# Attention with mixed heads and a gated feed-forward: Keys loaded three places further ahead, and two of four score evictions on VectorE

## The chip, the cores and the metric

The kernel runs on one core of one Trainium2 chip. The metric is the device time in microseconds (us) of one execution, and the time before is the median of 3 runs: 1879.54 us (1875.44 to 1880.68).

## What is computed

Eight batches of 448 tokens with 12 heads of 64. Scores are mixed over the heads before the softmax, and its result is mixed over the heads again before it meets the Values. The attention's output, 3584 rows of 768, goes through a feed-forward layer with a gate.

```python
scores = scale * np.matmul(q, k.transpose(0, 1, 3, 2))
scores = np.einsum('bhij,hg->bgij', scores, w_pre)
scores = scores - np.max(scores, axis=-1, keepdims=True)
attn = np.exp(scores)
attn = attn / (np.sum(attn, axis=-1, keepdims=True) + 1e-09)
attn = np.einsum('bhij,hg->bgij', attn, w_post)
out = np.matmul(attn, v)
x = out.transpose(0, 2, 1, 3).reshape(B * S, H * D)
h = x @ w_in
g = h - np.tanh(h)
return g @ w_out
```

## The kernel before

The kernel has two stages. In the attention stage each batch's 448 queries are four blocks (120, 120, 120 and 88 rows), and each block is cut into groups of ten queries. A group has 120 rows, one for each of its queries and each head, so that both mixes over heads are matmuls with a block-diagonal matrix of 120 x 120. Two groups at a time make a *place*: the stage is a loop of some 180 places (`for p in range(NPL + 3)`), each of which does this:

- **gather**: SyncE issues two DMAs (line 496) that collect the scores of two groups from the tile `s` into tiles `t`, for two places later. `t` has three buffers for even groups and two for odd ones.
- **issue** (line 370): behind the gathers SyncE issues up to six DMAs that wait in a list: loads of Queries, Keys and Values, stores of finished x, and, last, chunks of the weights that are being converted. A load that is put on the list in one place is issued in the next one. SyncE issues in order and waits in order.
- **premix** (lines 512 to 517): TensorE mixes two groups into two banks `ps_p`, the second one from a high part `th` and a low part `tl` of `t`.
- **norm** (541 to 545): VectorE takes the reciprocals of the last place's sums, ScalarE scales the mix matrix by them (`wr`).
- **split** (504, 505): VectorE casts the next place's odd group to `th`, GpSimd makes `tl`.
- **expo** (527, 529): VectorE's maxima, behind the cast in its order, and ScalarE's exponentials `e`. They release `ps_p` for the next premix.
- **jobs of this place**, from the table `todo`: transposes of Keys (`prep_k`, line 415) or Queries (`prep_q`, 441) on TensorE, values (line 598), or the scores of two pairs of heads (line 475). All of them share four banks `ps_m`. Their evictions are put behind the exponentials: line 481 for scores, 426 and 427 for Keys, 454 and 456 for Queries.
- **mix** (557) of the last place; ScalarE evicts it into `at` (566) at the start of the next place.
- a step or two of the **conversion** of the weights (lines 80 to 104) on VectorE, ScalarE and GpSimd.

A fixed order is recorded for each engine; nothing is reordered at run time. Scores of one pair of heads fill two banks; `scores` is called for an even pair `hp` and then for the odd one, so that a score place fills four banks and has four evictions. Before, an even pair's go to ScalarE and VectorE, and an odd pair's both to ScalarE. The first 16 evictions name their engines themselves and are not touched.

The table `todo` is filled by a planner ahead of the loop. For each batch but the first it chooses three places `p` for the loads of Keys (four heads each, 448 KB, pieces of 256 bytes; two buffers `kr`) and for each a place `o` for its transposes: at least two places after `p`, never in a place with scores or transposed Queries, and for the second and third load not before the score places that free a buffer of the transposed Keys. The third load waits for the first one's transposes, whose buffer it takes. Loads and transposes come out of it as follows (place of load, place of transposes; the load is issued one place after its own), from place 0 on:

| batch | first | second | third |
|---|---|---|---|
| 1 | 5, 7 | 6, 11 | 8, 13 |
| 2 | 27, 30 | 28, 34 | 31, 36 |
| 3 | 50, 52 | 51, 56 | 53, 58 |
| 4 | 72, 75 | 73, 79 | 76, 81 |
| 5 | 95, 97 | 96, 101 | 98, 103 |
| 6 | 117, 120 | 118, 124 | 121, 126 |
| 7 | 140, 142 | 141, 146 | 143, 148 |

The Values of the next batch are loaded at the places around these (in batch 2 at 26, 27 and 28), as are a Query block and the store of x.

The second stage is the feed-forward layer (lines 249 to 321), which the change does not touch.

Of the kernel before, what the change touches and what calls it, by code (L numbers as in the profile page):

```python
# [148 lines left out]
def kernel_body(  # L149
# [11 lines left out]
    nc = tc.nc  # L161
# [121 lines left out]
    def parts_gate(r):  # L283
        z = r.shape[1]
        gh = ff.gp.tile([P, TB], F32R, name="gh", tag="gh")
        gl = ff.gp.tile([P, TB], F32R, name="gl", tag="gl")
        nc.scalar.copy(gh[:, :z], r)  # L287
        nc.vector.tensor_sub(gl[:, :z], r, raw(gh[:, :z]))  # L288
        return gh, gl
# [47 lines left out]
    with ExitStack() as st:  # L337
# [16 lines left out]
        blocks = [(b, m) for b in range(B) for m in range(NM)]  # L354
# [110 lines left out]
        def scores(i, hp, engines=None):  # L465

            b, m = blocks[i]
            n = sizes[m]
            if hp == 0:
                sts[i] = sp.tile([MT, H, S], F32, name="s", tag="s")  # L470
            (qh, ql), (kh, kl) = qbs[i], kks[b, hp // 2]
            pss = [ps_m.tile([P, 512], F32, name="ps_q", tag="ps_m") for _ in halves]
            for x, (qx, kx) in enumerate(((qh, kh), (qh, kl), (ql, kh))):
                for a, ps in zip(halves, pss):
                    nc.tensor.matmul(ps[:n, :S], qx[a, hp, :], kx[a, hp % 2], start=(x == 0), stop=(x == 2))  # L475

            def rest():

                two = engines or (nc.scalar.copy, nc.scalar.copy if hp % 2 else nc.vector.tensor_copy)
                for j, (eng, ps) in enumerate(zip(two, pss)):  # L480
                    eng(sts[i][:n, 2 * hp + j, :], ps[:n, :S])

            sooner.append(rest)
# [252 lines left out]
        first = [t for t, (i, g) in enumerate(groups) if g == 0] + [NG, NG, NG]  # L736
        todo = {p: [] for p in range(NPL + 8)}

        def at_place(p, *job):
            todo[p].append(job)  # L740
# [13 lines left out]
        at_s, p, kind = {}, 0, None  # L754
# [18 lines left out]
        for i, (b, m) in enumerate(blocks):  # L773
            p0 = first[i] // 2
            if i + 2 < len(blocks):
                p = at_s[i + 2, 0] - 1
# [5 lines left out]
                for hq in range(NP // 2):  # L782
                    at_place(p0 + 4 + hq, load_v, b, hq)
        for b in range(1, B):
            p, o, done = first[blocks.index((b - 1, 1))] // 2 - 1, 0, []
            for hq in range(3):
                if hq == 2:

                    p = max(p, done[0] + 1)
                at_place(p, load_k, b, hq)  # L790
                o = max(p + 2, o + 1)
                p += 1
                if hq > KB - 4:

                    o = max(o, at_s[blocks.index((b - 1, 3)), hq - 1 - (KB - 4)] + 1)
                for r in range(2):
                    while any(f is scores or f is prep_q for f, *a in todo[o]):
                        o += 1
                    at_place(o, prep_k, b, 2 * hq + r)
                done.append(o)  # L800
                assert o < at_s[blocks.index((b, 0)), hq], (b, hq)
# [69 lines left out]
    for n in range(N):  # L871
        b, f = n // NF, n % NF
# [13 lines left out]
        if n + 3 == N:  # L886
            done = {n + 1: [parts_gate(gates.pop(n + 1))]}
# [48 lines left out]
```

## Time and profile before

| | |
|---|---|
| median of 3 runs | 1879.54 us (1875.44 to 1880.68) |
| the profiled execution, its own time | 1880.95 us |
| its span, first to last instruction | 1879.2 us |
| mean granted TensorE clock | 0.998 of full speed |
| attention stage, first premix to the last mix | 24 to 936 us |
| feed-forward stage | 936 to 1879 us |

The profile is of one execution. Busy time is given by engine: PE is TensorE's matmuls, PEld its loads of weights, DVE VectorE, ACT ScalarE, POOL GpSimd, SP SyncE; SPq are the DMAs that SyncE issues. An arrow names what an engine waited for by engine, tile and line; a wait for several things is put down to the one that came last by the profile, and where the engine named had long been done, it was another, often a DMA. Matmuls are pipelined, and their ends are modelled. Rows of a timeline begin with start and length in us; rows of stretches have the window, its length, the busy times of PE, PEld, DVE, ACT and POOL with their instructions, the granted clock, the DMA engines' share and GB/s.

### The profile page before, as it was taken

The numbers are of one execution on the slowest core, as the hardware profiler recorded it, in microseconds if no ns is written. First come the engines' busy times: TensorE is split into PE (matmuls) and PEld (weight loads), VectorE is DVE, ScalarE is ACT, GpSimd is POOL, SyncE is SP. The second block draws the span as 40 slices with busy tenths as digits, with TensorE's granted clock in tenths as the row PEclk, the third lists the DMA queues.
The fourth block names the chain that finished last, engine by engine and source line by source line (L and its number), as shares of the span: only waits on it lengthen the run. The fifth ranks groups of instructions, "written<-read, shape, count | busy, mean of one in ns | idle before, by whom it ended". The sixth has DMA issues, their size and how long they took to land.

```text
span 1879.2 us, 35344 instructions
## 1 busy us (share of the span) xinstructions
PE 1851.1 (99%) x13150; PEld 1525.9 (81%) x13150; DVE 1184.7 (63%) x2457; ACT 1133.8 (60%) x2503; POOL 451.9 (24%) x401
## 2 busy tenths in 40 slices
PE   8999999999999999999999999999999999999998
PEld 6777887787878777877788888888888888888887
DVE  5676766767776676766456556556566566565555
ACT  5787887878888788788634443434434434433433
POOL 2344444444444345444201000000000000000000
PEclk9999999999999999999999999999999999999999
DMA  6667658676675757656565565665655655655651
GB/s 162 183 183 201 189 166 221 182 208 190 177 216 171 209 177 205 195 164 189 212 255 193 206 246 192 223 218 196 235 213 196 235 205 196 237 209 191 233 193 42
DMA packets 232795, 371.92 MB, mean 198 GB/s; under 512 B 98992, under 2 KB 207536, under 8 KB 218288
## 3 DMA queue, kind: packets, MB, share of 16 engines
q1 hardware_dynamic: 231740, 368.45, 60.5%
q8 instruction: 104, 1.70, 0.4%
q10 hardware_dynamic: 884, 1.22, 0.2%
q14 instruction: 67, 0.55, 0.1%
HBM read 245.37 MB, written 47.19 MB: 156 GB/s over the span
## 4 chain that ended last, share of the span: by engine, by line
PE 86%; DMA 6%; ACT 3%; DVE 2%; issue 2%; POOL 1%; SPq 0%; ACTq 0%; POOLq 0%; DVEq 0%
PE ps_o L557 13%; PE ps_h L256 8%; PE ps_h L260 8%; PE ps_h L255 8%; PE ps_m L598 7%; PE ps_p L512 6%; PE ps_q L475 6%; PE ya L303 5%; PE ya L300 5%; PE ya L301 5%; DMA t<-s 4%; PE yb L303 3%; PE yb L301 3%; PE yb L300 3%; PE ps_p L517 2%
## 5 line engine op out<-in xcount | busy, mean ns | idle before, releaser
L557 PEld LDWEIGHTS ps_o<-wr,e 120*112 120x112 f32 (+1 forms) x2880 | 307.2, 177 | 49.8 <-issue 30.1
L557 PE MATMUL ps_o<-wr,e 120*112 120x120 f32 (+1 forms) x2880 | 340.5, 271 | 4.1 <-ACT wr L545 4.1
L527 DVE TENSOR_REDUCE mx<-ps_p 120x1 f32<-120x448 f32 x360 | 218.6, 622 | 136.9 <-PE ps_p L512 136.7
L505 POOL TENSOR_TENSOR tl<-t,th 120x448 fp32r<-120x448 f32 x179 | 204.4, 1142 | 391.8 <-DVE th L504 221.5
L287 ACT CAST gh<-r 128x512 fp32r<-128x512 f32 x112 | 69.6, 621 | 373.3 <-DVE r L280 373.3
L256 PE MATMUL ps_h<-xl,w 128*128 128x512 f32 x672 | 263.2, 392 | 0.5 <-POOL pad L222 0.5
L255 PE MATMUL ps_h<-xh,w 128*128 128x512 f32 x672 | 262.8, 391 | 0.0
L529 ACT ACTIVATE e<-ps_p,mx 120x448 f32<-120x448 f32 x360 | 225.8, 636 | 36.7 <-DVE mx L527 36.1
L245 POOL TENSOR_TENSOR xl<-rx,xh 128x512 fp32r<-128x512 f32 x38 | 53.7, 1415 | 741.3 <-ACT xh L244 741.3
L566 ACT COPY at<-ps_o 112x960 f32<-112x960 f32 x156 | 154.5, 990 | 113.4 <-PE ps_o L557 112.5
L303 PE MATMUL ya<-w,gl 128*128 128x512 f32 x448 | 177.1, 395 | 0.7 <-DVE gl L288 0.7
L276 DVE SCALAR_TENSOR_TENSOR r<-qa,ps_h 128x512 f32<-128x512 f32 x112 | 77.0, 687 | 158.7 <-ACT t L273 158.7
L300 PE MATMUL ya<-w,gh 128*128 128x512 f32 x448 | 175.0, 391 | 1.3 <-ACT gh L287 1.3
L301 PE MATMUL ya<-w,gh 128*128 128x512 f32 x448 | 174.9, 390 | 0.0
L260 PE MATMUL ps_h<-xh,w 128*128 128x512 f32 x672 | 170.5, 389 | 0.0
L512 PE MATMUL ps_p<-t,wpre 120*120 120x448 f32 x360 | 165.7, 542 | 4.3 <-ACT e L529 3.5
L598 PE MATMUL ps_m<-at,vr 112*64 112x120 f32 (+1 forms) x3072 | 163.3, 263 | 1.9 <-ACT at L566 1.5
L598 PEld LDWEIGHTS ps_m<-at,vr 112*64 112x64 f32 x3072 | 149.7, 138 | 14.7 <-ACT at L566 3.7
L270 ACT ACTIVATE u<-ps_h 128x512 f32<-128x512 f32 x112 | 66.9, 597 | 149.2 <-PE ps_h L260 149.2
L260 PEld LDWEIGHTS ps_h<-xh,w 128*128 128x128 f32 x672 | 126.1, 188 | 26.2
L256 PEld LDWEIGHTS ps_h<-xl,w 128*128 128x128 f32 x672 | 126.6, 188 | 24.6 <-POOL pad L222 0.9
L255 PEld LDWEIGHTS ps_h<-xh,w 128*128 128x128 f32 x672 | 126.6, 188 | 22.9
(102 smaller groups left out, 3622.0 us busy)
## 6 DMA issues: line engine op xcount, KB each, us to landing
w<-ws SPq DMA_DIRECT2D x112, 1536.0 KB
t<-s SPq DMA_DIRECT2D x342, 210.0 KB
cr<-in_moe_w_in_dram SPq DMA_DIRECT2D x24, 512.0 KB
cr<-in_moe_w_out_dram SPq DMA_DIRECT2D x32, 384.0 KB
vr<-in_v_dram SPq DMA_DIRECT2D x24, 448.0 KB
kr<-in_k_dram SPq DMA_DIRECT2D x23, 448.0 KB
out_dram<-ob SPq DMA_DIRECT2D x24, 384.0 KB
qr<-in_q_dram SPq DMA_DIRECT2D x23, 360.0 KB
```

Source lines behind the costliest of these rows:

```text
L255: nc.tensor.matmul(ph, wh[:, fs], xh, start=(c == 0), stop=False)
L256: nc.tensor.matmul(ph, wh[:, fs], xl, start=False, stop=False)
L260: nc.tensor.matmul(ph, wl[:, fs], xh, start=False, stop=(c == NK - 1))
L300: nc.tensor.matmul(y, gh[:, tok], wh[:, es], start=first, stop=False)
L301: nc.tensor.matmul(y, gh[:, tok], wl[:, es], start=False, stop=False)
L303: nc.tensor.matmul(y, gl[:, tok], wh[:, es], start=False, stop=last)
L505: eng.tensor_sub(tl[:n, :], x[:n, :], raw(th[:n, :]))
L512: nc.tensor.matmul(pa[:n, :], wpre[:n, :n], tg.pop(2 * p)[:n, :], start=True, stop=True)
L527: nc.vector.tensor_reduce(out=mx[:n, :], in_=ps[:n, :], axis=AX.X, op=ALU.max, negate=True)
L529: nc.scalar.activation(e[:n, :], ps[:n, :], AF.Exp, bias=mx[:n, :], scale=1.0, accum_out=zs[:n, 0, j : j + 1])
L557: nc.tensor.matmul(ps[:CP, j, c * GP : (c + 1) * GP], e[:n, c * CP : (c + 1) * CP], wr[:n, j, :], start=True, stop=True,)
L598: nc.tensor.matmul(pv[j * D : (j + 1) * D, r, :n], vt[:, j, c, :], ats[i][:, c, 2 * hp + j, :n], start=(c == 0), stop=(c == NC - 1),)
```

## The change

The loads of Keys are planned from three places earlier, transposes come at least four places after their load, and an odd pair's second score eviction goes to VectorE.

```diff
             def rest():
-
-                two = engines or (nc.scalar.copy, nc.scalar.copy if hp % 2 else nc.vector.tensor_copy)
+                two = engines or (nc.scalar.copy, nc.vector.tensor_copy)
                 for j, (eng, ps) in enumerate(zip(two, pss)):
                     eng(sts[i][:n, 2 * hp + j, :], ps[:n, :S])
...
         for b in range(1, B):
-            p, o, done = first[blocks.index((b - 1, 1))] // 2 - 1, 0, []
+            p, o, done = first[blocks.index((b - 1, 1))] // 2 - 4, 0, []
             for hq in range(3):
                 if hq == 2:
                     p = max(p, done[0] + 1)
                 at_place(p, load_k, b, hq)
-                o = max(p + 2, o + 1)
+                o = max(p + 4, o + 1)
                 p += 1
```

The table becomes:

| batch | first | second | third |
|---|---|---|---|
| 1 | 2, 7 | 3, 11 | 8, 13 |
| 2 | 24, 28 | 25, 34 | 29, 36 |
| 3 | 47, 52 | 48, 56 | 53, 58 |
| 4 | 69, 73 | 70, 79 | 74, 81 |
| 5 | 92, 97 | 93, 101 | 98, 103 |
| 6 | 114, 118 | 115, 124 | 119, 126 |
| 7 | 137, 142 | 138, 146 | 143, 148 |

Of the transposes only the first ones of batches 2, 4 and 6 move. Lines from 479 on have one number less after the change (a blank line went).

SyncE near the start of the attention stage, before: `t` are gathers, `kr` Keys, `qr` a Query block, `cr` chunks of weights.

```order
L496 DMA t<-s 120x1x448 x14
L367 DMA qr<-in_q_dram 88x12x64
L367 DMA cr<-in_moe_w_in_dram 128x1024 x3
L496 DMA t<-s 120x1x448 x2
L367 DMA kr<-in_k_dram 112x16x64
L496 DMA t<-s 120x1x448 x2
L367 DMA kr<-in_k_dram 112x16x64
L496 DMA t<-s 120x1x448 x4
L367 DMA kr<-in_k_dram 112x16x64
```

The same stretch after:

```order
L495 DMA t<-s 120x1x448 x10
L367 DMA kr<-in_k_dram 112x16x64
L495 DMA t<-s 120x1x448 x2
L367 DMA kr<-in_k_dram 112x16x64
L495 DMA t<-s 120x1x448 x2
L367 DMA qr<-in_q_dram 88x12x64
L367 DMA cr<-in_moe_w_in_dram 128x1024 x3
L495 DMA t<-s 120x1x448 x8
L367 DMA kr<-in_k_dram 112x16x64
```

The first two Keys' loads of batch 1 now stand ahead of the Query block and the weights, and of two more pairs of gathers each; the third stands where it stood.

TensorE at place 28, before: premix (`ps_p`), mix (`ps_o`) and the next premix.

```order
L512 MATMUL ps_p<-t,wpre 120x448
L515 MATMUL ps_p<-th,wph 120x448
L516 MATMUL ps_p<-th,wpl 120x448
L517 MATMUL ps_p<-tl,wph 120x448
L557 MATMUL ps_o<-wr,e 112x120 x8
```

And after:

```order
L511 MATMUL ps_p<-t,wpre 120x448
L514 MATMUL ps_p<-th,wph 120x448
L515 MATMUL ps_p<-th,wpl 120x448
L516 MATMUL ps_p<-tl,wph 120x448
L415 MATMUL ps_m<-ident,kr 128x112 x8
L556 MATMUL ps_o<-wr,e 112x120 x8
```

The transposes of the first Keys of batch 2 came from place 30, where they stood ahead of that place's values.

VectorE in a score place, before: the maxima (`mx`), one eviction (`s`), two kinds of conversion steps, and the next place's normalisation (`zs`).

```order
L527 TENSOR_REDUCE mx<-ps_p 120x1 x2
L481 COPY s<-ps_q 120x448
L80 TENSOR_SCALAR cm<-cr 128x512 x2
L83 TENSOR_SCALAR cr<-cr 128x512 x2
L541 TENSOR_SCALAR zs<-zs 120x1 x2
```

And after:

```order
L526 TENSOR_REDUCE mx<-ps_p 120x1 x2
L480 COPY s<-ps_q 120x448 x2
L80 TENSOR_SCALAR cm<-cr 128x512 x2
L83 TENSOR_SCALAR cr<-cr 128x512 x2
L540 TENSOR_SCALAR zs<-zs 120x1 x2
```

A second eviction stands between the maxima and the conversion; on ScalarE two stand where three did.

## The prediction

> **What bounds the kernel now.** I read the page first. TensorE is busy for nearly the whole span, so what can be won is its idle time and any time at a lower clock.
>
> ```profile
> PE 1851.1 (99%) x13150; PEld 1525.9 (81%) x13150; DVE 1184.7 (63%) x2457; ACT 1133.8 (60%) x2503; POOL 451.9 (24%) x401
> ```
>
> Of 1879.2 us, 28.1 are idle. The waits of TensorE's matmuls, longest in total first, say for what:
>
> ```profile
> PE ps_o L557 <- ACT wr L545: 4.1, 7, 1.3
> PE ps_m L415 <- DMA kr<-in_k_dram: 3.9, 3, 1.4
> PE ps_p L512 <- ACT e L529: 3.5, 5, 0.9
> PE ps_m L415 <- ACT e L529: 3.3, 1, 3.3
> PE ps_m L598 <- ACT at L566: 1.5, 2, 1.3
> ```
>
> Columns: us in total, times, longest. L415 is the transposes of Keys; four of their waits, 7.2 us together, are the two rows with L415. The row of 3.3 names an exponential of ScalarE, which the transposes do not need: they need banks that earlier evictions have emptied, and Keys in SBUF. A wait for several things is put down to the one seen last, so I take it for the load as well. TensorE's timeline around it (start, us, then the idle time in brackets):
>
> ```profile
> 52.74 0.92 PE L512 MATMUL ps_p<-t,wpre 120*120 120x448 f32 x2
> ...
> 57.53 1.73 PE L415 MATMUL ps_m<-ident,kr 112*128 112x112 f32 x8 [3.26 <-ACT e L529]
> 59.18 4.84 PE L598 MATMUL ps_m<-at,vr 112*64 112x120 f32 x48
> ...
> 65.68 0.92 PE L512 MATMUL ps_p<-t,wpre 120*120 120x448 f32 x2
> ```
>
> Four batches later the same work of one place (premix, transposes, values, mix) met its Keys in time:
>
> ```profile
> 516.41 0.92 PE L512 MATMUL ps_p<-t,wpre 120*120 120x448 f32 x2
> ...
> 518.64 2.68 PE L598 MATMUL ps_m<-at,vr 112*64 112x120 f32 x48
> ...
> 522.98 0.92 PE L512 MATMUL ps_p<-t,wpre 120*120 120x448 f32 x2
> ```
>
> From premix to premix that is 65.68 - 52.74 = 12.94 us against 522.98 - 516.41 = 6.57: the late Keys cost 6.37, of which 3.26 is the gap. The rest is the clock, as the stretches show (after POOL's busy time come the granted clock, the DMA share and GB/s):
>
> ```profile
> 57.00:64.00 7.00, 6.47 (x57) 6.07 (x57) 2.26 (x5) 3.28 (x8) 0.39 (x1) 0.53 0.70 170
> 64.00:70.00 6.00, 6.00 (x49) 4.87 (x48) 4.44 (x11) 4.10 (x10) 1.13 (x1) 1.00 0.21 70
> 280.00:290.00 10.00, 8.58 (x65) 6.62 (x62) 6.96 (x20) 7.57 (x20) 3.71 (x3) 1.00 1.08 267
> 740.00:750.00 10.00, 8.93 (x82) 6.93 (x77) 6.45 (x19) 8.93 (x22) 5.09 (x5) 1.00 1.00 259
> ```
>
> After the gap of 3.26 us the clock was 0.53 for 7 us; at the shorter gaps (up to 1.4 us, at 289 and 749 us) it stayed 1.00. The Trainium skill, "TensorE: Matmul & The Clock Gate", Part 1, says that the clock halves after an idle window of about 3.4 us that runs freely, so that a gap of this size may or may not trip it. The trace agrees that it can; in a run where it does not, the time before would be about 3 us shorter, and the time after the same.
>
> **Part 1, the loads.** Before, SyncE issued the second batch's first Keys behind a Query block and three chunks of weights:
>
> ```profile
> 43.83 0.62 SPq L367 DMA_DIRECT2D qr<-in_q_dram  x1
> 44.50 1.65 SPq L367 DMA_DIRECT2D cr<-in_moe_w_in_dram  x3
> ...
> 48.00 0.65 SPq L367 DMA_DIRECT2D kr<-in_k_dram  x1
> ```
>
> They were awaited at 57.53, 9.5 us later. In the new order two Keys' loads stand ahead of that Query block, and there are four places to the transposes, some 18 us at the 4.59 us of a score place (below); some places are shorter. For the later batches the load leaves the crowded stretch (with Values, Query, and the write of x) for one three places earlier:
>
> ```profile
> 170.00:180.00 10.00, 10.00 (x101) 8.11 (x100) 5.75 (x16) 8.25 (x22) 4.51 (x5) 1.00 1.09 237
> 150.00:160.00 10.00, 10.00 (x106) 8.24 (x108) 6.76 (x19) 7.81 (x21) 4.29 (x4) 1.00 0.49 147
> ...
> 380.00:390.00 10.00, 10.00 (x108) 8.11 (x106) 5.93 (x19) 8.37 (x21) 4.28 (x4) 1.00 0.38 133
> ```
>
> There the DMA engines are at 0.38 to 0.49 instead of 1.00 to 1.09. In the even batches the first transposes also move two places up, so their distance grows by one place only; three places after its issue are some 14 us, and 9.5 was enough in the crowded stretch. So all four waits go: 3.26 + 3.9 = 7.2 us, and 12.94 - 6.57 - 3.26 = 3.1 us of halved clock. Sum 10.3.
>
> Is something else late next at 54 us? Its neighbours:
>
> ```profile
> 55.73 0.39 DVE L504 CAST th<-t 120x448 fp32r<-120x448 f32 x1 [2.90 <-DMA t<-s]
> 56.26 1.13 POOL L505 TENSOR_TENSOR tl<-t,th 120x448 fp32r<-120x448 f32 x1 [6.38 <-DVE th L504]
> 57.38 0.62 ACT L529 ACTIVATE e<-ps_p,mx 120x448 f32<-120x448 f32 x1
> ```
>
> The gather was late as well, but the next premix, at 52.74 + 6.57 = 59.31, finds its operand (56.26 + 1.13 = 57.39) and its bank (57.38 + 0.62 = 58.00) ready. Nothing takes the place of the wait.
>
> What the moved loads cost where they now stand: each is ahead of the next two gathers in SyncE's order, and a late gather holds VectorE at L504:
>
> ```profile
> DVE th L504 <- DMA t<-s: 50.2, 25, 5.6
> ```
>
> That is 2.0 us a time. TensorE's non-Keys waits are 4.1 + 3.5 + 1.5 = 9.1 us, so at most 18% of those 50.2 us can have reached it. 17 loads move (two a batch in seven batches, and the third of the three even ones by two places). From below: nothing, as with third Keys' loads, of which five already stand by themselves and left TensorE busy through the 14 us behind each; one of these, and one of the two that did not:
>
> ```profile
> 189.11:203.11 14.00, 14.00 (x127) 11.27 (x125) 11.49 (x30) 13.18 (x34) 5.57 (x6) 1.00 0.86 239
> 299.49:313.49 14.00, 12.85 (x122) 10.32 (x120) 9.39 (x23) 9.79 (x24) 7.71 (x7) 1.00 0.83 214
> ```
>
> From above: 17 x 2.0 x 0.18 = 6.1 us at the trace's own share, 34 if all of it passed. I take 0, since the other loads that made 299 us hard are no neighbours any more; the old places lose the same number of loads.
>
> The transposes that move (batches 2, 4, 6) come into a place without values, where ScalarE's two casts have less room. Seven such places (the second Keys of a batch) exist already; two had a wait behind them:
>
> ```profile
> 313.47 0.36 PE L557 MATMUL ps_o<-wr,e 120*112 120x120 f32 x1 [1.15 <-ACT wr L545]
> 542.87 0.64 PE L512 MATMUL ps_p<-t,wpre 120*120 120x448 f32 x1 [0.40 <-ACT e L529]
> ```
>
> So 3 x (1.15 + 0.40) / 7 = 0.7 us, between 0 and 3 x 1.15 = 3.5. I take 0.7.
>
> **Part 2, the evictions.** Eight score places use a pair of engines of their own; 92 others now send the second odd eviction to VectorE.
>
> ```profile
> L481 ACT COPY s<-ps_q 120x448 f32<-120x448 f32 (+1 forms) x284 | 132.3, 544 | 6.5 <-PE ps_q L475 6.2
> L481 DVE COPY s<-ps_q 120x448 f32<-120x448 f32 (+1 forms) x100 | 62.0, 621 | 16.8 <-PE ps_q L475 16.3 <-DMA ws<-cs 0.4
> ```
>
> ScalarE loses 132.3 / 284 = 0.47 us of busy time a score place, VectorE gains 0.62 (92 x 0.62 = 57 us). The Trainium skill, "VectorE: DVE Perf Modes", Specifications, puts ScalarE closer to PSUM and VectorE closer to SBUF, which speaks against this half; the rows agree, 544 ns against 621. Who has room is read from two score places, premix to premix:
>
> ```profile
> 112.91:117.50 4.59, 4.59 (x34) 3.47 (x33) 2.97 (x8) 4.59 (x13) 4.13 (x4) 1.00 0.96 234
> 342.89:347.48 4.59, 4.59 (x34) 3.47 (x33) 2.97 (x9) 4.59 (x12) 1.77 (x3) 1.00 1.00 223
> ```
>
> ScalarE has none (4.59 of 4.59), VectorE is at 2.97 and goes to 3.6. The cost of 57 us is thus covered by VectorE's idle time there. Behind both places TensorE waited for ScalarE:
>
> ```profile
> 118.56 0.36 PE L557 MATMUL ps_o<-wr,e 120*112 120x120 f32 x1 [0.48 <-ACT wr L545]
> 348.43 0.36 PE L557 MATMUL ps_o<-wr,e 120*112 120x120 f32 x1 [0.38 <-ACT wr L545]
> ```
>
> 0.47 us less on ScalarE ends such waits: 0.48 + 0.38 = 0.9. Two more waits stood where Keys and Values were loaded together:
>
> ```profile
> 186.36 0.64 PE L512 MATMUL ps_p<-t,wpre 120*120 120x448 f32 x1 [0.65 <-ACT e L529]
> 647.18 0.64 PE L512 MATMUL ps_p<-t,wpre 120*120 120x448 f32 x1 [0.95 <-ACT e L529]
> ```
>
> With the Keys gone from there I count these 1.6 as won, too. So 2.5 us of the 9.1; the bounds are 0 and 9.1.
>
> **Sum.** The profiled execution took 1880.95 us (span 1879.2, and 1.75 around it), 1.4 above the median of 1879.54. 1880.95 - 10.3 - 2.5 + 0.7 = 1868.85, so 1868.9 us. I leave the 1.4 out: what differs between the runs (1875.44 to 1880.68) is of the size of the clock's 3.1 us, which the change ends.
>
> **Rivals.** (a) *The loads only move the collision.* The Keys land in time, but the gathers behind the 17 of them come late, VectorE stands at L504, its maxima and ScalarE's exponentials slip, and premix waits. For it: score places and places with values of 4.6 to 5.8 us now follow the loads, no longer ones. Against it: the row at 189.11. At 18% it gives 1880.95 - 10.3 + 6.1 = 1876.8. If all 34 us passed it would be 1880.95 - 10.3 + 34 = 1904.7, slower. It ends the gain from 10.3 / 34 = 30% on, and is slower by 0.3% from (10.3 + 5.6) / 34 = 47% on. Chance 15%; 4 of these slower.
> (b) *VectorE becomes the bound in score places.* Its order is in sequence: two evictions stand ahead of the next normalisation, cast and maximum. For it: 3.6 of 4.59 us is a mean of engines that wait for each other. If a third of the 0.62 us came through at 92 places it would be 92 x 0.2 = 18 us: 1880.95 - 10.3 + 18 = 1888.7. Against it: ScalarE at 4.59 of 4.59 lost under 0.5 us a time. Chance 4%.
> (c) *The loads are not early enough in the even batches.* Then the gap of 1.44 us at 636 stays: 1870.3. Chance 4%; inside the range.
>
> **Numbers.** A difference of 0.3%, 5.6 us, is about what a measurement of this kernel can tell: faster is under 1873.9, slower over 1885.1. Forecast with (c): 81%, a few of these above 1873.9. Range: the low end if all 9.1 us of other waits go, 1880.95 - 10.3 - 9.1 = 1861.6; the high end is rival (a) at its 18% with the 0.7 of the transposes, 1877.5. So 1862 to 1877.5. Faster 0.77, same 0.16, slower 0.07.
>
> **What would show it.** Right: no wait of L415 for kr, the place at 53 us 6.6 us long, clock 1.00 from 50 to 70 us, L481 at 192 copies each on ScalarE and VectorE, the matmuls' waits for wr shorter. Wrong: L504 waiting for t well over 50.2 us and L512 waiting for e over 5 us (a), or score places longer than 4.6 us with VectorE at their length (b).

## The result, and the profile after

The changed kernel took 1861.18 us, the median of 4 runs (1859.88 to 1861.98), against 1877.49 (1875.19 to 1880.68) for the kernel before: a ratio of 0.9911, 95% interval 0.9892 to 0.993. That is faster, as forecast, and 0.8 us under the low end of the range (1862.0). The forecast was a gain of 12.1 us on the profiled execution. By the medians the gain is 16.3 us. Between the two profiled executions it is 21.0 (spans of 1879.2 and 1858.2 us), but that sets an execution of before that is slower than its median beside the fastest of the changed kernel.

The page's engine row of the profile after (the one of before stands in the prediction):

```profile
PE 1844.0 (99%) x13150; PEld 1523.0 (82%) x13150; DVE 1230.1 (66%) x2549; ACT 1099.2 (59%) x2411; POOL 455.4 (25%) x401
```

TensorE's idle time fell from 28.1 to 1858.2 - 1844.0 = 14.2 us. Its busy time fell as well, by 7.1 us, though it issued the same 13150 matmuls: 3.1 us of it by the prediction's reading is time at half the clock. The other 4.0 I take for waits that the view of busy time does not show as idle.

The matmuls' waits after (lines from 479 on have one number less):

```profile
PE ya L300 <- ACT gh L287: 1.9, 2, 1.0
PE ps_o L556 <- ACT wr L544: 1.6, 2, 1.3
PE ps_b L658 <- POOL ident masks.py:199: 1.5, 1, 1.5
PE ps_p L511 <- ACT e L528: 0.9, 1, 0.9
```

No transposes (L415) wait for Keys any more. Of the 9.1 us of other waits in the attention stage (for `wr`, `e` and `at`) 2.5 are left: the two rows with `ps_o` and `ps_p`. All but 0.3 of that are two waits, of 0.9 us at the stage's second place and 1.3 at its end, that stood there before as well.

TensorE's timeline at the place that took 12.94 us before:

```profile
53.06 0.92 PE L511 MATMUL ps_p<-t,wpre 120*120 120x448 f32 x2
...
54.43 0.93 PE L415 MATMUL ps_m<-ident,kr 112*128 112x112 f32 x8
55.29 2.68 PE L597 MATMUL ps_m<-at,vr 112*64 112x120 f32 x48
...
59.63 0.92 PE L511 MATMUL ps_p<-t,wpre 120*120 120x448 f32 x2
```

59.63 - 53.06 = 6.57 us, and no idle time in front of the transposes. (The first two Keys' loads passed three pairs of gathers each, not the two that the description of the change gives.) The clock over the same stretches as before:

```profile
57.00:64.00 7.00, 7.00 (x67) 5.72 (x64) 6.42 (x16) 6.50 (x17) 2.22 (x2) 1.00 0.18 71
64.00:70.00 6.00, 6.00 (x75) 5.24 (x74) 5.21 (x17) 3.99 (x11) 3.94 (x4) 1.00 0.69 187
```

It is 1.00 where it was 0.53. VectorE's wait for the gathers, and the score evictions by engine:

```profile
DVE th L503 <- DMA t<-s: 28.1, 19, 3.4
```

```profile
L480 DVE COPY s<-ps_q 120x448 f32<-120x448 f32 (+1 forms) x192 | 116.9, 621 | 16.1 <-PE ps_q L475 14.9 <-DMA ws<-cs 0.4 <-DMA cr<-in_moe_w_in_dram 0.2
L480 ACT COPY s<-ps_q 120x448 f32<-120x448 f32 (+1 forms) x192 | 92.4, 537 | 6.5 <-PE ps_q L475 6.2
```

The waits for gathers went down from 50.2 to 28.1 us. I had taken them to stay as they were, and had feared that they would grow. Both parts of the change lowered them: the loads alone to 37.5 (38.8 in a second profile), the evictions alone to 39.3.

```profile
DVE th L504 <- DMA t<-s: 37.5, 24, 5.3
DVE th L504 <- DMA t<-s: 39.3, 18, 5.5
```

Comparing both profiles place by place (premix to premix, same work) gives three groups. K: the four places that waited for Keys (7, 52, 120, 142), 10.9 us. L: nine late places (31, 56, 76, 101, 102, 103, 121, 165, 166), 7.6 us. Seven of these stand behind the crowded loads of Keys. Places 165 and 166, with 1.2 us, do not: they begin at 863 us, and the last load of Keys is issued at 759.7, so near them only Values, a Query block, a store of x and weights are moved. A: six places where ScalarE was late (13, 18, 24, 63, 86, 153), 1.8 us. The rest is small change, the moved transposes among it.

### The profile page after: what moved, and what is told of

It reads as the page before. It is cut to its first block, busy times and chain, and to the rows that moved or that the text cites. A ratio compares the mean times of both kernels' runs of the same rounds, so it can differ in the third digit from the quotient of the medians.

```text
span 1858.2 us, 35351 instructions
## 1 busy us (share of the span) xinstructions
PE 1844.0 (99%) x13150; PEld 1523.0 (82%) x13150; DVE 1230.1 (66%) x2549; ACT 1099.2 (59%) x2411; POOL 455.4 (25%) x401
## 4 chain that ended last, share of the span: by engine, by line
PE 95%; DMA 2%; ACT 1%; DVE 1%; issue 1%; POOL 0%; SPq 0%; ACTq 0%; POOLq 0%
PE ps_o L556 17%; PE ps_m L597 8%; PE ps_h L256 8%; PE ps_h L260 8%; PE ps_h L255 8%; PE ps_p L511 7%; PE ps_q L475 7%; PE ya L303 5%; PE ya L300 5%; PE ya L301 5%; PE yb L303 3%; PE yb L301 3%; PE yb L300 3%; PE ps_p L516 2%; PE ps_p L514 2%; PE ps_p L515 2%
## 5 line engine op out<-in xcount | busy, mean ns | idle before, releaser
L504 POOL TENSOR_TENSOR tl<-t,th 120x448 fp32r<-120x448 f32 x179 | 204.6, 1143 | 378.9 <-DVE th L503 194.0
```

The lines of the kernel that those rows point to most:

```text
L504: eng.tensor_sub(tl[:n, :], x[:n, :], raw(th[:n, :]))
```

## The experiments

Theory P was that the moved loads themselves end K and L by emptying the crowded stretch. Theory E, the rival, was that ScalarE's new room absorbs late gathers, so that the evictions end L.

**Loads alone.** The diff of the change without its first hunk:

```diff
-            p, o, done = first[blocks.index((b - 1, 1))] // 2 - 1, 0, []
+            p, o, done = first[blocks.index((b - 1, 1))] // 2 - 4, 0, []
-                o = max(p + 2, o + 1)
+                o = max(p + 4, o + 1)
```

> The loads and transposes of the change, with the score evictions as before (ScalarE three, VectorE one). The place-by-place comparison of the two profiles gives three groups: K, the four places that waited for Keys (10.9 us with the slow clock); L, nine places that were late behind the crowded loads (7.6 us); A, six score places in which ScalarE was late (1.8 us). Theory P (the moved loads empty the crowded stretch): K and L go, A stays: 1861.2 + 1.8 = 1863 us. Theory E (ScalarE's new slack absorbs late gathers): only K goes, L and A stay: 1861.2 + 9.4 = 1870.6 us.

Measured 1864.23 us (5 runs, 1864.17 to 1865.34), ratio 0.9918 (0.9905 to 0.9931). P had 1863, E 1870.6. The loads carry most of the gain. In its profile places 31, 56, 76, 101 and 121 of group L are within 0.1 us of the shortest that any profile shows for them; 103, 120 and 165 are still 0.18, 0.85 and 0.54 us over the changed kernel's, and group A is all there.

**Evictions alone.**

```diff
-                two = engines or (nc.scalar.copy, nc.scalar.copy if hp % 2 else nc.vector.tensor_copy)
+                two = engines or (nc.scalar.copy, nc.vector.tensor_copy)
```

> The evictions of the change, with Keys planned as before. Theory P: only group A goes, 1877.5 - 1.8 = 1875.7 us, and the late places behind the crowded loads are still late. Theory E: A and L go, 1877.5 - 9.4 = 1868.1 us. Both: the waits of the transposes for Keys stay, 7 us of them.

Measured 1876.63 us (12 runs, 1871.09 to 1880.24) beside 1880.92 on the same chip, ratio 0.9972 (0.9959 to 0.9984): 5.3 us by the ratio, 4.3 by the medians, between P's 1.8 and E's 9.4. The profiled execution was the slowest of the 12 (1880.24), so its places tell where the time goes and not how much is won. Matmul waits of its profile:

```profile
PE ps_m L415 <- DMA kr<-in_k_dram: 8.0, 4, 4.3
PE ps_p L512 <- ACT e L529: 5.3, 5, 1.9
PE ps_o L557 <- ACT wr L545: 1.5, 2, 1.3
```

The waits for `wr` went from 4.1 to 1.5, so group A ended, and place 56 of L with it (1.40 us, a wait for `wr` too). Places 165 and 166 ended as well (1.2 us). That makes 1.8 + 1.4 + 1.2 = 4.4 us. The waits for `e`, which I take to come from late gathers, did not shrink (3.5 before), and the Keys' waits stayed. Places 31 and 121, behind the loads, took 1.3 and 0.8 us more than in the profile of before. So E holds for the places that ended here, and not for late gathers behind the loads.

**Both, and loads alone, on one chip.** The next four ran together.

> The changed kernel once more, on the same chip as the next three. Its four times lay within 2.1 us (1859.88 to 1861.98), where 22 executions of the kernel before spread over 12. Theory: with no wait for Keys there is nothing left that differs from run to run, so 1861 us within 1.5, and a profile with no place over its floor.

> Loads alone, on the same chip as the changed kernel. What lies between the two is what the evictions are worth once the loads are early. By the places that were over their floor with loads alone (0.33 + 0.43 + 0.14 + 0.38 + 0.26 + 0.26 where ScalarE was full, 0.85 + 0.58 + 0.54 + 0.32 + 0.18 elsewhere, less 0.24): 4.0 us, so 1865. If the evictions only relieved the waits that I had counted (0.48 + 0.38), 0.9 us: 1862.

The changed kernel: 1862.35 us (4 runs, 1862.16 to 1863.01), ratio 0.9911 (0.9898 to 0.9923); a few of its places were over the floor (0.92 at place 79, 0.57 at 31), so the expectation's "no place" was wrong. Loads alone: 1865.57 (5 runs), ratio 0.9928 (0.9916 to 0.994). Between them are 3.2 us, nearer the 4.0 that the places gave than the 0.9 of my prediction. In the two profiles 2.7 us of the difference lie in the attention stage; another 1.8 lie in the feed-forward layer, which the change does not touch, with a clock drop at its start (below). One of the waits that stay with loads alone, and below it the totals of that profile:

```profile
112.72 0.36 PE L557 MATMUL ps_o<-wr,e 120*112 120x120 f32 x1 [0.48 <-ACT wr L545]
```

```profile
PE ps_o L557 <- ACT wr L545: 3.0, 6, 1.3
PE ps_p L512 <- ACT e L529: 1.8, 3, 0.9
```

In the changed kernel the mix of that place begins without one:

```profile
111.74 0.36 PE L556 MATMUL ps_o<-wr,e 120*112 120x120 f32 x1
```

**A third eviction on VectorE** (with the change's loads):

```diff
-                two = engines or (nc.scalar.copy, nc.scalar.copy if hp % 2 else nc.vector.tensor_copy)
+                two = engines or (nc.vector.tensor_copy if hp % 2 else nc.scalar.copy, nc.vector.tensor_copy)
```

> The change with a third score eviction on VectorE: an even pair's go to ScalarE and VectorE, an odd pair's both to VectorE. Theory (room): VectorE has 2.97 of 4.59 us in a score place before, 3.6 with two evictions, 4.2 with three; still under the place, and TensorE stays the bound: 1861 to 1864 us. Rival (VectorE in order): with three evictions between its maxima and the next cast it is late at most score places, 92 x 0.2 = 18 us: 1879 us or more.

Measured 1864.78 us (5 runs), 2.4 more than the changed kernel beside it, ratio 0.9922 (0.991 to 0.9933). The rival's 1879 is far off: VectorE does not become the bound. But it comes near. The same score place (17), premix to premix, in the changed kernel:

```profile
106.52:111.11 4.59, 4.59 (x34) 3.47 (x33) 4.35 (x10) 4.59 (x12) 3.77 (x3) 1.00 0.98 229
```

And with three evictions:

```profile
106.04:110.63 4.59, 4.59 (x34) 3.47 (x33) 4.55 (x12) 4.17 (x10) 3.77 (x3) 1.00 0.98 220
```

VectorE, third of the busy times, goes from 4.35 to 4.55 of 4.59 us. What is late then is still ScalarE, which waits for a conversion step that VectorE has put off, and holds its own mix matrix back:

```profile
109.33 0.68 ACT L85 ACTIVATE cr<-cr 128x512 f32<-128x512 int32 x1 [0.28 <-DVE cr L83]
109.91 0.96 ACT L566 COPY at<-ps_o 112x960 f32<-112x960 f32 x1
110.77 0.67 ACT L545 ACTIVATE wr<-wpost,zs 120x120 f32<-120x120 f32 x2
```

The matmuls' waits for `wr` are 3.7 us here, against 2.2 in the changed kernel beside it. Not all of the 2.4 us are the evictions': in this profile the stretch behind the last premix was 950.1 us long against 947.9, with a clock drop at the start of the feed-forward layer (949.7 with the same drop in the second run of loads alone):

```profile
960.00:964.00 4.00, 3.78 (x10) 3.02 (x11) 3.25 (x7) 1.12 (x3) 0.00 (x0) 0.57 0.01 3
```

Two and two is the better split here, though the margin is small.

**Distance without lead** (with the evictions): the first two Keys of each batch stay in the crowd, and the first ones' transposes come six or seven places after their load. The third load, which follows these transposes, leaves the crowd (place 12 for 8, 35 for 31).

```diff
-                two = engines or (nc.scalar.copy, nc.scalar.copy if hp % 2 else nc.vector.tensor_copy)
+                two = engines or (nc.scalar.copy, nc.vector.tensor_copy)
-                o = max(p + 2, o + 1)
+                o = max(p + 4, o + 1)
```

> The evictions and the distance of four places, but the loads planned from where they were before: Keys are issued beside Values, Query and x, and the transposes come six places after the load. Theory (crowding): the waits for Keys go (7 us and their slow clock), but the late gathers behind the crowded loads stay, places 31, 76 and 121 above all (2.7 us in the profile of before, 4.9 with evictions alone): 1864 to 1866 us. Rival (only the distance matters): as the changed kernel, 1861 us, and no late place.

Measured 1868.21 us (6 runs, 1866.86 to 1870.87), 5.9 more than the changed kernel beside it, ratio 0.9942 (0.9929 to 0.9954); the rival is out. No matmul waits for Keys, but these waits stay:

```profile
PE ps_p L512 <- ACT e L529: 5.1, 5, 1.3
PE ps_o L557 <- ACT wr L545: 3.0, 4, 1.3
```

The waits for gathers stay near those of before: 46.8 us at L504, against 28 to 29 in the three profiles of the changed kernel:

```profile
DVE th L504 <- DMA t<-s: 46.8, 20, 5.8
```

One of these places in it, at 165 to 180 us:

```profile
165.00:180.00 15.00, 13.79 (x131) 11.07 (x128) 8.27 (x20) 8.79 (x23) 5.02 (x5) 1.00 0.94 260
```

And the same stretch of the changed kernel, where nothing is lost:

```profile
165.00:180.00 15.00, 15.00 (x139) 12.11 (x140) 10.34 (x28) 11.03 (x28) 6.52 (x6) 1.00 0.91 241
```

This points to the term that I had too small: with the Keys' own waits ended in both, getting two of three loads out of the crowd is worth up to 5.9 us to others. 4.6 us over the changed kernel stand at places 31, 75, 76, 120 and 121, in the old crowd. The figure is not clean, since the transposes, and the third loads behind them, stand elsewhere too (places 54 to 56 and 145 to 147 are 3.8 us over, while the places that the transposes left are shorter). The DMA engines are nearly as busy in both stretches (0.94 and 0.91); what differs by the order of issue is which transfers the gathers stand behind.

**Lead without distance** (with the evictions): the loads go three places up, and the rule for the transposes stays at two places, so the first ones of the odd batches move up, too. They land three places after their load (places 47 and 50 in batch 3), since the place two after it has scores; the even batches' stay at four, as in the changed kernel. The expectations speak of two places; here no transposes stand that close behind their load.

```diff
-            p, o, done = first[blocks.index((b - 1, 1))] // 2 - 1, 0, []
+            p, o, done = first[blocks.index((b - 1, 1))] // 2 - 4, 0, []
-                two = engines or (nc.scalar.copy, nc.scalar.copy if hp % 2 else nc.vector.tensor_copy)
+                two = engines or (nc.scalar.copy, nc.vector.tensor_copy)
```

> Loads three places earlier and the evictions of the change, but transposes two places after their load as before: in the odd batches the first ones follow their load by two places, in an emptier stretch. Theory (crowding): a load takes some 5 us outside the crowd, two places are about 8, so hardly any wait for Keys: 1862 to 1864 us. Rival (distance): the odd batches' first transposes wait again, 1 to 3 us each at four places, one of them with the clock's 3 us: 1868 to 1872 us.

> Lead and evictions without the distance, now on the same chip as the changed kernel of the next run. Its median of 1859.98 was the lowest so far, on another chip; its profile (1863.91) had 3.8 us of stage more than that of the changed kernel. Theory: the distance is worth nothing once the loads are out of the crowd, and the two agree within 1 us. Rival: the third load, which follows the first transposes, comes back nearer to Values and costs 2 us or more.

> The changed kernel beside the run without the distance, on the same chip: 1861 to 1862.4 us, as in its two series so far. Theory: equal to the run beside it within 1 us; rival: 2 us or more below it.

The first series gave 1859.98 us (4 runs, 1859.73 to 1863.91), ratio 0.9888 (0.9866 to 0.9909). The second 1861.72 (5 runs), ratio 0.9913 (0.9899 to 0.9927), beside 1861.85 for the changed kernel, ratio 0.991 (0.9896 to 0.9924). No transposes wait for Keys in either profile. On one chip the two agree within 0.2 us: out of the crowd three places are enough, and the five of the changed kernel's odd batches are worth nothing that can be measured. With the lead two places were not tried. No version that was run beats the changed kernel clearly.

**Transposes unmoved**: the change, with the first transposes of the even batches left where they were.

```diff
-                o = max(p + 4, o + 1)
+                o = max(p + (6 if hq == 0 and b % 2 == 0 else 4), o + 1)
```

> The change with the first transposes of batches 2, 4 and 6 left at their old places (30, 75, 120), and so their third load too: TensorE's order is that of before. My prediction charged 0.7 us for moving them: then this is 0.7 faster than the changed kernel, 1861.5 on the chip of the last runs. By the places of the two profiles the move is worth 0.5 less at one place and 0.8 more at the other in favour of the move, 3 x 0.24 = 0.7 us: then it is 0.7 slower, 1863.

Measured 1860.92 us (4 runs), ratio 0.9889 (0.9866 to 0.9912), beside the first series without distance (1859.98) and no run of the changed kernel. Its interval overlaps the changed kernel's; a difference of 0.7 us either way is below what these runs can tell, and stays open. In its profile places 28, 73 and 118 are 0.53 us shorter than the changed kernel's and 30, 75 and 120 0.77 longer, with no new wait at the latter.

**The first batch alone**: lead and distance for the second batch (number 1) only, the evictions as before.

```diff
-            p, o, done = first[blocks.index((b - 1, 1))] // 2 - 1, 0, []
+            p, o, done = first[blocks.index((b - 1, 1))] // 2 - (4 if b == 1 else 1), 0, []
-                o = max(p + 2, o + 1)
+                o = max(p + (4 if b == 1 else 2), o + 1)
```

> Only the second batch's Keys (number 1) are loaded earlier; all else as before. If the gap of 3.26 us and the 3.1 us of halved clock behind it are as read, 6.4 us less than the profiled execution of before (1880.95), so 1874.6; against the median of 1877.5 it is 6.4 less if each execution has the slow clock (1871.1), and about 3.3 to 4.8 if half of them have not (1872.7 to 1874.2).

Measured 1874.59 us (11 runs, 1871.47 to 1879.84) beside 1880.92, ratio 0.9971 (0.9959 to 0.9983): 6.3 us by the medians, 5.5 by the ratio, against 6.4 read from one place of one profile. Its profile also shows how uncertain group L is: only 2.3 us of it were left, against 7.6 and 8.1 in the two profiles of before (all three over the changed kernel's places), though the later batches' Keys stood in the crowd as ever. So what the crowd costs is not the same in each execution. In this profile the wait at place 52 was longer than before, and now took the clock along:

```profile
284.25 0.38 PE L415 MATMUL ps_m<-ident,kr 112*128 112x112 f32 x2 [3.10 <-DMA kr<-in_k_dram]
```

```profile
284.00:289.00 5.00, 4.75 (x52) 4.50 (x54) 1.25 (x2) 2.16 (x4) 1.89 (x2) 0.66 0.91 265
```

**Before, once more.**

> The kernel before, unchanged, profiled once more. Its four times fell in two pairs, near 1880 and near 1875.3. Theory clock: the pairs differ by whether the gap at 54 us trips the clock; an execution near 1875 shows no window under 1.00 from 57 to 64 us and is about 3 to 5 us shorter. Rival: the clock drops in each, and the pairs differ in other waits (gathers).

It took 1879.21 us. The gap at place 7 was 2.66 us, and the clock dropped again, for half as long:

```profile
57.64 0.96 PE L415 MATMUL ps_m<-ident,kr 112*128 112x112 f32 x8 [2.66 <-DMA kr<-in_k_dram]
```

```profile
58.00:62.00 4.00, 4.00 (x43) 3.86 (x43) 1.48 (x3) 2.40 (x6) 0.00 (x0) 0.58 0.97 240
62.00:66.00 4.00, 4.00 (x38) 3.12 (x35) 1.79 (x6) 1.26 (x3) 1.13 (x1) 0.99 0.04 15
```

With 22 executions of before on that chip, from 1872.63 to 1884.6 us, the idea of two pairs falls: the times do not fall into two groups. Whether the clock stays up in the fastest executions is open, since none of them was profiled. How long each Keys' wait is, and how long the slow clock behind it lasts, differed between the profiles. The series of kernels without late Keys lie closer (1.2 and 2.9 us with loads alone, 0.9 to 3.6 for the changed kernel, at most 4.2 in the others), but they have 4 to 6 runs each.

## Why the prediction was wrong

**Waits for Keys, 7.2 us, and 3.1 us of halved clock: right.** All four waits are gone, place 7 takes the 6.57 us foretold, the clock is 1.00. By places the group is 10.9 us against 10.3. Done for one batch only, it gave 6.3 by the medians (5.5 by the ratio), against 6.4. In the second profile of before the slow clock behind place 7 lasted half as long, so the 3.1 are not there in full each time.

**"So 2.5 us of the 9.1": wrong; this is the term of the sum that was mis-sized.** Two things were too small in it. I counted 1.6 us as won where Keys and Values were loaded together, by two rows. And I counted 0.9 us for the evictions, by two rows again. The runs on one chip give both parts: loads alone won 1879.8 - 1865.57 = 14.2 us, where the prediction had 10.3 + 1.6 - 0.7 = 11.2, and the evictions another 3.2 (2.7 in the attention stage of the two profiles), where it had 0.9. Together that is 17.4 us against 12.1. On another chip loads alone won 16.7 by the medians. That the loads' part comes from the crowd is supported by the run of distance without lead (up to 5.9 us), also at places behind it, where premix waits for `e`; its exact size stays open.

Of the 9.1 us of waits 6.6 went. Even all 9.1 would not have been all of it: TensorE's busy time fell by 7.1 us, of which 3.1 is the clock. The other 4.0 I could not have read from the matmuls' idle time. The Trainium skill, "Trainium Kernel Development and Optimization", Performance Expectations, calls matmul busy time a bad measure of how close a kernel is to roofline, since matmuls are pipelined; here it was a bad measure of what can be won, by these 4.0 us. The time from premix to premix of equal places has them in it, and I used that view for one place only.

**0.7 us charged for the moved transposes: not seen.** The move changes places 28 and 30 by +0.53 and -0.77 us (73 and 75, 118 and 120 likewise). Undoing it gave a time within the spread of the changed kernel's runs, in a series without that kernel.

**0 for the moved loads where they now stand: right.** Their bound, 6.1 us in the trace's own share, was rival (a). With the loads alone the waits for gathers fell by 12.7 us; there was no such collision.

**"Nothing takes the place of the wait": right.** VectorE had room for the second eviction, so rival (b) did not come. It had less room than I said, though. Of the two score places that I forecast at 3.6 us the second came to 3.66 and the first (place 17, above) to 4.35:

```profile
332.04:336.63 4.59, 4.59 (x34) 3.47 (x33) 3.66 (x11) 4.33 (x11) 1.35 (x2) 1.00 1.00 220
```

In place 17 the cast took 0.49 us before, behind a wait of 0.59; now it takes 1.17 without a wait. The traces do not say why.

```profile
116.22 0.49 DVE L504 CAST th<-t 120x448 fp32r<-120x448 f32 x1 [0.59 <-DMA t<-s]
110.02 1.17 DVE L503 CAST th<-t 120x448 fp32r<-120x448 f32 x1
```

With three evictions VectorE is at 4.55 of 4.59 us, and 2.4 us are lost, not 18. (Four score places have engines of their own, with eight pairs of heads, and not eight as I wrote; the 92 others are right.)

**Distance:** I gave it a part in ending the waits, and rival (c) rested on it. Either does it by itself: with the loads in the crowd, six places ended all waits for Keys (distance without lead); with the loads early, three places did. On top of the lead more distance brings nothing that can be measured.

**The base: wrong.** I started from the profiled execution and left out that it was 1.4 us above the median shown. With four runs it was 3.5 above (1880.95 against 1877.49). The forecast of 1868.9 is 7.7 us over the measured 1861.18: 3.5 of these are the base, and 4.2 the size of the gain (16.3 by the medians against 12.1). From the median as base the same sum would have given 1865.4, with a low end of 1877.49 - 10.3 - 9.1 = 1858.1; from the 1879.54 known then the low end would have been 1860.1. So the term above alone would not have put the time below the range; it took the base as well.

## What to carry to other kernels

When a transfer is moved out of a crowded stretch, price what it does to the others in that stretch as well as its own wait; a run with the wait ended but the crowd kept (distance without lead) helps to separate the two. Subtract a forecast gain from the median of several runs, and not from the one execution that was profiled. In a bound engine's loop compare equal pieces of work by the time from start to start, since idle time leaves out slow clock, and whatever else a matmul that counts as busy is held up by. An engine that is busy for all of a place is worth relieving even if only a few waits name it, as long as the one that takes over keeps some room.

## What the runs showed of the hardware

Each single gap of 2.2 us or more in TensorE's work was followed by a lower clock in these profiles: 3.26 us (before), 3.10 (first batch alone), 2.66 (before again) were each followed by windows at 0.53 to 0.66. In the run with evictions alone one of 4.31 was followed by 0.52 from 57 to 64 us, and one of 2.21 by 0.66:

```profile
291.49 0.29 PE L415 MATMUL ps_m<-ident,kr 112*128 112x112 f32 x1 [2.21 <-DMA kr<-in_k_dram]
```

```profile
292.00:297.00 5.00, 5.00 (x56) 4.70 (x55) 1.39 (x3) 2.06 (x4) 1.33 (x2) 0.66 0.90 267
```

Single gaps of 1.42 us (before, 1.00 from 289 to 296 us) and 1.91 us (evictions alone) left it at 1.00:

```profile
187.54 0.64 PE L512 MATMUL ps_p<-t,wpre 120*120 120x448 f32 x1 [1.91 <-ACT e L529]
187.00:194.00 7.00, 6.46 (x76) 5.71 (x77) 6.83 (x19) 6.58 (x18) 4.63 (x5) 1.00 0.52 125
```

Two shorter gaps close together were followed by it, too. With the third eviction on VectorE they were 1.29 and 0.66 us, ahead of the stretch at 0.57 shown above:

```profile
958.83 0.50 PE L300 MATMUL ya<-w,gh 128*128 128x512 f32 x1 [1.29 <-ACT gh L287]
960.22 0.79 PE L303 MATMUL ya<-w,gl 128*128 128x512 f32 x1 [0.66 <-DVE gl L288]
```

In the second run of loads alone 1.01 and 0.66 us were followed by 0.66 from 962 to 967 us; in the changed kernel 0.97 and 0.65 at the same matmuls left the clock at 1.00. The rule cited in the prediction (the Trainium skill, "TensorE: Matmul & The Clock Gate", Part 1) has an idle window of about 3.4 us; by these rows well under 3 us of idle time can be enough.

The same evictions of 120 x 448 take VectorE 621 ns, whether it does 100 or 192 of them, and ScalarE 544 and 537.
